# Transposes by DMA, smaller term buffers, deferred phi(q) and a fuller scheduler model in a two-layer attention kernel

## The chip, the cores and the metric

The kernel runs on one core of one Trainium2 chip. The metric is the device time of one execution in microseconds (us). All times are medians of several executions, with the lowest and highest in brackets where they matter.

The engines are named as in the profile: PE is TensorE (matmuls), PEld its weight loads, DVE is VectorE, ACT is ScalarE, POOL is GpSimd and SP the engine that issues DMAs here.

## The reference

Four blocks with residuals, A, B, A, B, on x of 2,048 rows by 512 columns in bf16:

```python
def _A_ref(x, wq, wk, wv, wo):        # 32 heads of 16, one shared key and value
    q = split_heads(x @ wq); k = x @ wk; v = x @ wv
    p = _softmax(q k^T * 16 ** -0.5)
    return merge_heads(p v) @ wo
def _B_ref(x, wqkv, wo):              # linear attention
    phi = lambda t: jnp.where(t > 0, t + 1, jnp.exp(t)) + 1e-6
    pq, pk = phi(q), phi(k)
    kv = einsum(pk, v); z = sum(pk)
    return merge_heads((pq kv) / (pq z + 1e-6)) @ wo
x = x + _A_ref(_layernorm(x), ...); x = x + _B_ref(_layernorm(x), ...)   # twice
```

(Notation shortened, meaning unchanged.) One A and the B after it are called a layer here. The softmax is nearly all of the work: 32 x 2,048 x 2,048 exponentials a layer, which the kernel cuts into 2,048 "positions" of 128 keys by 512 queries.

## The kernel before

The program orders its own instructions. Every operation is registered with an estimated duration, a priority, its buffers and the engines that may run it. A list scheduler plays the whole kernel through in a model at build time and writes down the order for each engine. The chip then follows that order, with semaphores.

The parts that matter (cuts marked by `# ...`):

```python
# the steady stage: two PSUM bank sets for ACT (banks 0-2 and 3-4), banks 5 and 6 for DVE,
# bank 7 for the accumulator; everything else ("misc") shares bank 6
def for_misc():
    # ...
    return (6, 5, 4, 3) if ctl.ramp else (6,)

# ACT: two or three positions by one exponential
oe = add(AC, tac(m * 512), lambda e: e.activation(PTA[...], bank(3 * s, m * 512), ACTF.Exp, scale=SCALE), ...)

# DVE: one position at a time out of PSUM (P1), then three shifted copies of four positions (xo);
# value matmuls with all four terms add up to the exponential
o = add(DV, tdv(512), lambda e: e.tensor_scalar(out=PTD[:, hp.idx, 0, i * 512:(i + 1) * 512], in0=bank(db), ...), name="P1")
dep = [add(DV, tdv(512 * m, 0.26), lambda e, r=r: e.tensor_scalar(out=PTD[:, hp.idx, r, 0:512 * m],
           in0=PTD[:, hp.idx, 0, 0:512 * m], scalar1=float(SHIFT[r]), ...), name="xo")]
# PTD: three buffers of 16 KB a partition, one for a group of four positions; free when all 16 matmuls are done

# layer norm, and the attention output likewise (otr, otc): transpose on PE, copy out of bank 6
o = add(PE, 0.22, tr, ..., acq=[hb], name="tr")                      # four 128x128 transposes
o2 = add((DV, AC), {...}, cp, uses=[hb], rel=[hb], name="xnT")       # copy to SBUF

# phi = max(t, 0) + min(exp t, 1): ACT, then DVE and POOL, then POOL adds
def phi(h, o, dst, keys, prio, tiled=False):
    o1 = add(AC, ..., ACTF.Exp, name="phe")
    o2 = add(DV, ..., op0=ALU.max, op1=ALU.add, name="phr")
    o3 = add(PO, PHM, ..., op0=ALU.min, op1=ALU.max, name="phm")
    add(PO, PHS, ..., op=ALU.add, name="phs")
```

The softmax here doesn't subtract the row's maximum and nothing guards it: scores larger than these inputs give would overflow.

## Time and profile before

1,659.47 us (1,656.86 to 1,660.10, three runs). From the timeline of ACT I cut the profiled execution (span 1,650.1 us) into five stages, at the first run of unbroken exponentials, at the end of the last exponential of each layer and at the first of the next.

| stage | us |
|---|---|
| start | 39.4 |
| plateau of layer one | 744.9 |
| change of layer | 54.3 |
| plateau of layer two | 760.2 |
| end | 51.3 |

In the lines of the groups view, the number after `x` is the count. After the first bar come the busy time of the group in us and the mean duration of one instruction in ns. After the second bar comes the idle time of the engine just before them, and what ended it. A line of the waits view reads: who waited, for whom, us in total, times, longest wait.

```profile
ACT PTA L845 <- PE ps_all L689: 62.7, 79, 10.5
DVE PTD L895 <- PE ps_all L689: 126.8, 222, 1.5
```

These are the two waits: ACT's exponential and DVE's conversion, each waiting for its score matmul.

### The profile page before, as it was taken

The numbers are of one execution on the slowest core, as the hardware profiler recorded it, in microseconds if no ns is written. First come the engines' busy times: TensorE is split into PE (matmuls) and PEld (weight loads), VectorE is DVE, ScalarE is ACT, GpSimd is POOL, SyncE is SP. The second block draws the span as 40 slices with busy tenths as digits, with TensorE's granted clock in tenths as the row PEclk, the third lists the DMA queues.
The fourth block names the chain that finished last, engine by engine and source line by source line (L and its number), as shares of the span: only waits on it lengthen the run. The fifth ranks groups of instructions, "written<-read, shape, count | busy, mean of one in ns | idle before, by whom it ended". The sixth has DMA issues, their size and how long they took to land.

```text
span 1650.1 us, 41487 instructions
## 1 busy us (share of the span) xinstructions
PE 1575.9 (96%) x18511; PEld 530.1 (32%) x18511; DVE 1434.9 (87%) x2536; ACT 1521.9 (92%) x1495; POOL 172.7 (10%) x222
## 2 busy tenths in 40 slices
PE   6999999999999899999799999999999998999998
PEld 4322223222333223333452232233223232333334
DVE  6999888899898889988689988888999988988976
ACT  6999999999999799999589999999999997999986
POOL 3000000100010101112210000001000102011131
PEclk9999999999999899999899999999999999999999
DMA  4000000000000000000000000000000000000001
GB/s 131 1 1 1 2 1 2 1 1 1 2 1 1 1 1 1 1 2 2 2 4 1 1 1 2 1 1 2 1 1 1 1 2 1 2 1 1 2 2 54
DMA packets 7779, 10.03 MB, mean 6 GB/s; under 512 B 1456, under 2 KB 7088, under 8 KB 7600
## 3 DMA queue, kind: packets, MB, share of 16 engines
q1 hardware_dynamic: 7600, 7.37, 1.4%
q8 instruction: 145, 2.38, 0.6%
q14 instruction: 34, 0.28, 0.1%
HBM read 5.28 MB, written 2.10 MB: 4 GB/s over the span
## 4 chain that ended last, share of the span: by engine, by line
PE 59%; ACT 20%; DVE 19%; issue 1%; DMA 0%; POOL 0%; SPq 0%
PE ps_all L689 23%; PE ps_all L726 23%; ACT PTA L845 19%; PE ps_all L460 10%; DVE PTD L895 7%; DVE PTD L912 6%; PE ps_all L747 2%; DVE Eo L738 1%; DVE e_buf L1022 1%; DVE stats L513 1%; PE ps_all L531 1%; DMA x_sb<-in_A_x_dram 0%; ACT e_buf L1021 0%; DVE v_tok L1042 0%; PE ps_all L997 0%
## 5 line engine op out<-in xcount | busy, mean ns | idle before, releaser
L845 ACT ACTIVATE PTA<-ps_all 128x1536 bf16<-128x1536 f32 (+1 forms) x1231 | 1422.9, 1276 | 66.9 <-PE ps_all L689 62.7
L895 DVE TENSOR_SCALAR PTD<-ps_all 128x512 uint16<-128x512 f32 x1005 | 680.6, 684 | 132.2 <-PE ps_all L689 126.8
L689 PE MATMUL ps_all<-QT,Kr 32*128 32x512 bf16 x4152 | 709.0, 384 | 22.4 <-ACT PTA L845 8.8
L726 PE MATMUL ps_all<-PTD,Vaug 128*32 128x512 bf16 x4020 | 584.6, 388 | 9.4 <-DVE Eo L738 7.2
L726 PE MATMUL ps_all<-PTA,Vaug 128*32 128x512 bf16 x3091 | 545.7, 388 | 0.7 <-ACT PTA L845 0.6
L912 DVE TENSOR_SCALAR PTD<-PTD 128x2048 uint16<-128x2048 uint16 x756 | 518.4, 704 | 4.7
L689 PEld LDWEIGHTS ps_all<-QT,Kr 32*128 32x128 bf16 x4152 | 176.5, 91 | 522.5 <-ACT PTA L845 214.0
L726 PEld LDWEIGHTS ps_all<-PTD,Vaug 128*32 128x32 bf16 x4020 | 143.5, 94 | 197.1 <-issue 127.5
L726 PEld LDWEIGHTS ps_all<-PTA,Vaug 128*32 128x32 bf16 x3091 | 132.0, 94 | 201.1 <-issue 169.7
L1024 POOL TENSOR_SCALAR e_buf<-e_buf 128x512 f32<-128x512 f32 x64 | 42.2, 660 | 597.6 <-ACT e_buf L1021 597.6
L521 POOL TENSOR_TENSOR rstd<-veps,mhalf 128x1 f32<-128x1 f32 x27 | 23.6, 873 | 743.9 <-DVE veps L519 733.9
L460 PE MATMUL ps_all<-wqkv_sb,xnT 128*32 128x512 bf16 x1024 | 85.1, 397 | 1.3 <-ACT xnT L537 0.8
L1022 DVE TENSOR_SCALAR e_buf<-ps_all 128x512 f32<-128x512 f32 x64 | 43.8, 684 | 21.9 <-ACT e_buf L1021 21.8
L1021 ACT ACTIVATE e_buf<-ps_all 128x512 f32<-128x512 f32 x64 | 39.9, 624 | 11.4 <-PE ps_all L460 8.7
L747 PE MATMUL ps_all<-identf,Eo 128*128 128x128 f32 x256 | 44.3, 298 | 5.6 <-DVE OT L1003 2.6
L460 PE MATMUL ps_all<-xnT,wq_sb 128*32 128x128 bf16 (+1 forms) x896 | 43.5, 303 | 5.2 <-issue 4.2
L513 DVE BATCH_NORM_STATS2 stats<-x_sb 128x6 f32<-128x512 bf16 x64 | 42.9, 679 | 4.5 <-DMA x_sb<-in_A_x_dram 2.9
L1027 POOL TENSOR_TENSOR pk_tok<-e_buf 128x512 bf16<-128x512 f32 x32 | 43.6, 1364 | 15.2 <-DVE e_buf L1022 15.0
L1027 POOL TENSOR_TENSOR pqT<-e_buf 128x512 bf16<-128x512 f32 x32 | 42.9, 1340 | 21.9 <-DVE e_buf L1022 21.2
L738 DVE COPY Eo<-ps_all 128x512 f32<-128x512 f32 x62 | 42.3, 682 | 2.8 <-PE ps_all L747 1.6
L460 PE MATMUL ps_all<-wo_sb,OT 128*32 128x512 bf16 x512 | 42.2, 382 | 1.7 <-issue 0.8
L460 PE MATMUL ps_all<-xnT,wqkv_sb 128*32 128x128 bf16 (+1 forms) x896 | 40.7, 292 | 0.6 <-DVE e_buf L1022 0.4
(83 smaller groups left out, 740.2 us busy)
## 6 DMA issues: line engine op xcount, KB each, us to landing
out_dram<-x_sb SPq DMA_DIRECT2D x16, 128.0 KB, 1.7
x_sb<-in_A_x_dram SPq DMA_DIRECT2D x3, 512.0 KB, 7.0
wqkv_sb<-in_B_wqkv_dram SPq DMA_DIRECT2D x1, 1536.0 KB, 11.9
x_sb<-in_A_x_dram SPq DMA_DIRECT2D x2, 256.0 KB, 3.3
wq_sb<-in_A_wq_dram SPq DMA_DIRECT2D x1, 512.0 KB, 5.1
wo_sb<-in_A_wo_dram SPq DMA_DIRECT2D x1, 512.0 KB, 8.6
wo_sb<-in_B_wo_dram SPq DMA_DIRECT2D x1, 512.0 KB, 11.4
wk_sb<-in_A_wk_dram SPq DMA_DIRECT2D x1, 16.0 KB, 2.6
```

The lines of the kernel that those rows point to most:

```text
L460: i = e.matmul(out[32 * c:32 * c + 32], lhsT=lhsT[:, 32 * c:32 * c + 32], rhs=rhs, start=start, stop=stop, skip_group_check=True)
L513: add(DV, tdv(512), lambda e: e.bn_stats(stats[:, t, 0:6], x_sb[:, t, :]), reads=[("x", t)], writes=[("st", t)], prio=prio, name="bn")
L689: x = e.matmul(bank(b0 + k), lhsT=Kr[r, m, kt * P:(kt + 1) * P], rhs=QT[r, self.units[u][0] % 2, gs, q0:q0 + n], start=True, stop=True)
L726: return e.matmul(ps[32 * c:32 * c + 32, 7 * 512:8 * 512], lhsT=Vaug[:, kt, r, :], rhs=src, start=opened[0], stop=opened[1], skip_group_ch ...
L738: return (e.copy if oe.eng == AC else e.tensor_copy)(Eo[:, he.idx, :], bank(7))
L747: i = e.transpose(bank(ht.idx, P, qs * P), Eo[:, he.idx, qs * P:(qs + 1) * P], identf[:])
L845: oe = add(AC, tac(m * 512), lambda e: e.activation(PTA[:, hp.idx, 0:m * 512], bank(3 * s, m * 512), ACTF.Exp, scale=SCALE), deps=[o] + pr ...
L895: o = add(DV, tdv(512), lambda e: e.tensor_scalar(out=PTD[:, hp.idx, 0, i * 512:(i + 1) * 512], in0=bank(db), scalar1=SCALE * LOG2E * 128. ...
L912: dep = [add(DV, tdv(512 * m, 0.26), lambda e, r=r: e.tensor_scalar(out=PTD[:, hp.idx, r, 0:512 * m], in0=PTD[:, hp.idx, 0, 0:512 * m], sc ...
L1022: o2 = add(DV, tdv(512), lambda e: e.tensor_scalar(out=e_buf[:, hr.idx, :], in0=bank(h.idx), scalar1=0.0, scalar2=1e-6, op0=ALU.max, op1=A ...
L1024: o3 = add(PO, PHM, lambda e: e.tensor_scalar(out=e_buf[:, he.idx, :], in0=e_buf[:, he.idx, :], scalar1=1.0, scalar2=0.0, op0=ALU.min, op1 ...
L1027: add(PO, PHS, lambda e: e.tensor_tensor(out=dst, in0=sh(e_buf[:, hr.idx, :]), in1=sh(e_buf[:, he.idx, :]), op=ALU.add), deps=[o2, o3], us ...
```

## The change

It has several parts. Transposes in the plateau leave PE and bank 6 and become DMAs from SBUF to SBUF. The shifted terms get 4 KB buffers of their own, given back term by term, and at most two groups of four positions are open at once (it was three). The two limits do not count the same thing: before, a group was open until all its 16 value matmuls were done; now it counts as open only until its first buffer is free, and its shifted terms may live on. The phi(q) blocks of query block 2 (`b` = 2, counted from 0) wait until the layer's exponentials are done. At the layer ends, phi is done in two DVE steps instead of the POOL chain, half the residuals are added by DVE instead of an identity matmul, and small steps may go to ACT. wq is loaded behind six x tiles. The scheduler's model learns that DVE's wide instructions and POOL exclude each other (`port`), and how long loads take. Some twenty priorities and limits get new values.

```diff
+NT0 = 2
+NPD = 12
+LX = 0.338
-MP, AP, MF, AF = 1, 2.0, 0.4, 2.0
+AP = 0.904
+MF = 0.758
+AF = 2.764
+PCONT = 0.992
... (more priorities)
+            if e == DV and o.port and self.tfree[PO] > self.now + 1e-9 or e == PO and self.dport > self.now + 1e-9:
+                continue
...
-    PTD = sb("PTD", [P, NPD, NTERM, 2048], U16)
+    PTD = sb("PTD", [P, NPD, 2048], U16)
...
+        late = not (ctl.ramp or ctl.tail or ctl.hot())
+        if late:
+            tdma(lambda e: [e.dma_start(xnT[:, ft, t * P:(t + 1) * P], xn_buf[:, hx.idx, ft * P:(ft + 1) * P], transpose=True) for ft in range(FT)], ...)
+            return
...
+        if not (ctl.tail or ctl.hot()):
+            tdma(lambda e: [e.dma_start(OT[...], Osb[:, hos.idx, k, :], transpose=True) for k in range(4)], ...)
...
-            if not self.ramp and sum(not o.done for o in self.p1s) < DMIN:
+            if not self.ramp and sum(not o.done for o in self.p1s) < DMIN and not (sc.tfree[AC] + LAT[AC] - now < LX and not all(banks.free[a] for a, w in SETS)):
...
-                if not p_ptd.free:
+                if not p_ptd.free or self.n0 >= NT0:
...
+        fast = (ctl.tail or ctl.hot()) and not slow      # phi: min and add on DVE, then max and add on DVE
...
+                    if b >= PQF:
+                        ctl.later.append((b, g))
...
+        own = t % 4 < YD                                 # residual by DVE, no identity matmul
```

The `LX` line keeps DVE's next score matmul back when ACT is about to run dry.

## The prediction

> **What bounds the kernel now.** The program's instruction order is fixed at build time by a list scheduler with a cost model; the chip only executes that order. Each attention layer has 2,048 units of 128 keys by 512 queries to exponentiate ("positions"), 4,096 in all, shared between ACT (true exponential, two or three positions per instruction) and DVE (a bit-pattern approximation: one conversion out of PSUM, then three shifted copies for four positions). I first read the busy shares and the 40 slices of the page.
>
> ```profile
> PE 1575.9 (96%) x18511; PEld 530.1 (32%) x18511; DVE 1434.9 (87%) x2536; ACT 1521.9 (92%) x1495; POOL 172.7 (10%) x222
> ...
> ACT  6999999999999799999589999999999997999986
> ...
> PEclk9999999999999899999899999999999999999999
> ```
>
> The reader is to see that no engine is plainly the bound: PE, ACT and DVE are all nearly full, in two long plateaus (one a layer) with ACT at 90% or more, and that there are five holes: the start, slice 14, the change of layer (slices 20 and 21), slice 34, the end. Then the groups of instructions, shapes kept apart, for the price of one position.
>
> ```profile
> L845 ACT ACTIVATE PTA<-ps_all 128x1536 bf16<-128x1536 f32 x630 | 933.5, 1482 | 57.6 <-PE ps_all L689 53.7
> L895 DVE TENSOR_SCALAR PTD<-ps_all 128x512 uint16<-128x512 f32 x1005 | 680.6, 684 | 132.2 <-PE ps_all L689 126.8
> L845 ACT ACTIVATE PTA<-ps_all 128x1024 bf16<-128x1024 f32 x600 | 636.7, 1061 | 9.3 <-PE ps_all L689 9.0
> L912 DVE TENSOR_SCALAR PTD<-PTD 128x2048 uint16<-128x2048 uint16 x753 | 517.8, 706 | 4.7
> ```
>
> ACT did 3,091 positions in 1,423 us of union time: 0.46 us each. DVE did 1,005 at 0.684 + 0.75 x 0.706 = 1.21 us. If DVE gets x us free it takes x/1.21 positions over, each worth 0.46 us of ACT; the time falls by x(0.46/1.67) = **0.275x**. A microsecond freed on ACT is worth 0.725. The same lines show that DVE idles 127 us for score matmuls and ACT 63 us: both wait for PE and for PSUM banks. In the steady stage one bank (6) serves every projection, transpose and normalization, and is also one of only two that feed DVE's conversions.
>
> Two of the holes I opened with the windows view (columns: window, length, busy PE, PEld, DVE, ACT, POOL with counts, granted clock).
>
> ```profile
> 560.00:565.00 5.00, 3.72 (x37) 0.98 (x40) 4.70 (x8) 5.00 (x6) 1.07 (x3) 1.00 0.01 3
> 565.00:570.00 5.00, 2.39 (x21) 0.68 (x13) 3.46 (x5) 0.66 (x2) 3.28 (x3) 0.52 0.00 0
> 570.00:575.00 5.00, 2.84 (x16) 1.56 (x16) 2.60 (x6) 0.00 (x0) 0.00 (x0) 0.50 0.00 0
> ...
> 1385.00:1390.00 5.00, 2.81 (x11) 1.22 (x11) 4.28 (x9) 0.74 (x2) 2.13 (x2) 0.78 0.00 0
> 1390.00:1395.00 5.00, 4.49 (x35) 1.51 (x36) 3.38 (x8) 1.45 (x1) 0.00 (x0) 0.54 0.00 0
> ```
>
> ACT is empty for some 10 us and the clock falls to half. The timeline says with what:
>
> ```profile
> 564.77 1.27 POOL L1027 TENSOR_TENSOR pqT<-e_buf 128x512 bf16<-128x512 f32 x1 [0.35 <-DVE e_buf L1022]
> ...
> 568.03 2.95 DVE L912 TENSOR_SCALAR PTD<-PTD 128x2048 uint16<-128x2048 uint16 x3
> ...
> 568.20 1.63 POOL L1027 TENSOR_TENSOR pqT<-e_buf 128x512 bf16<-128x512 f32 x1 [0.61 <-DVE e_buf L1022]
> ...
> 571.37 0.71 PEld L747 LDWEIGHTS ps_all<-identf,Eo 128*128 128x128 f32 x4 [2.86 <-DVE OT L1003]
> ...
> 577.38 1.45 ACT L845 ACTIVATE PTA<-ps_all 128x1536 bf16<-128x1536 f32 x1 [10.49 <-PE ps_all L689]
> ```
>
> The four phi(q) blocks of query block 2 hold bank 6 one after another, each until ACT and DVE have read it; behind them wait an output transpose, its DVE copy, and the transpose that frees the accumulator's evacuation buffer. Between 561 and 573 us no attention-times-value matmul runs at all.
>
> **What the Trainium skill says.** "SBUF — State Buffer", Who interferes with whom: DVE in a two-port mode (or with two SBUF inputs) and GpSimd exclude each other for a whole instruction. The trace agrees in kind: the 2,048-wide shift has a median of 0.684 and a maximum of 1.752 us, and three of them took 2.95 us beside POOL's addition. "TensorE: Matmul & The Clock Gate", Part 1: the clock is half when the array was idle for about a window of 3.4 us; the trace has 0.52 and 0.50 there. "VectorE: DVE Perf Modes", The three transpose paths: a full 128x128 bf16 transpose is 390 ns on TensorE and 1,309 ns by DMA. Here a TensorE transpose shows 219 ns; no transposing DMA is in this trace, so its cost is untested. "TensorEngine Tiling (Array Packing)", Key Properties: a change of tiling mode drains TensorE. The trace agrees: weight loads of a new form come after gaps of 0.23 or 0.42 us laid to "issue".
>
> **The change part by part.**
>
> (1) *DMA transposes.* 27 normalizations take the POOL power path, which marks the steady ones, and 29 output transposes were copied by DVE: up to 56, less the few in the last ten positions. Each loses four PE matmuls (0.40 us as a block, and about 0.2 us of tiling switch: 0.6) and a DVE copy of 0.418 us, and leaves bank 6 free for some 1.5 us. DVE: 54 x 0.418 = 22.6 us. PE: 54 x 0.6 = 32 us. SP gets 54 x 4 = 216 DMAs; it is idle in the plateaus, and even at the new model's 5.1 us for four it would be busy 275 of 1,500 us. Their latency lies on a chain (normalize, project, linear attention state) that has tens of us to spare until the layer's end, where TensorE is kept.
>
> (2) *phi(q) of block 2 put off.* Four blocks a layer leave the plateau: 8 x 0.624 = 5.0 us of ACT (worth 0.725: 3.6) and 8 x 0.684 = 5.5 us of DVE. They come back between the last exponential and the second half of the normalization tiles, where ACT is 31% and DVE 54% busy (790 to 810 us); 64 more matmuls are 3.5 us of PE a layer at full clock. Mostly hidden, I allow +1 us a layer.
>
> (3) *Holes 14 and 34.* ACT busy was 37.8 of 50 us (530 to 580) and 50.3 of 60 (1350 to 1410), against 96% elsewhere: 10.2 + 7.4 = 17.6 us. Parts 1 and 2 remove exactly the work that blocks bank 6 there. I take **15 us**.
>
> (4) *Port and load model, 4 KB term buffers.* The same 48 KB become 12 buffers of 4 KB that come free term by term. The DVE lane never shows a wait for a term buffer, only for PE, so I give this nothing by itself. Choosing non-port work while POOL runs saves at most 753 x (0.706 - 0.684) = 17 us of DVE; I take 10.
>
> (5) *Steady sums.* DVE freed: 22.6 + 5.5 + 10 = 38 us, x 0.275 = **10.5 us**; ACT **3.6 us**. PE's 32 us and the free bank shorten the waits: outside the holes ACT waits some 40 us for scores and DVE some 110; I take a third of each, 13 x 0.725 + 37 x 0.275 = **20 us**.
>
> (6) *Layer ends.* In the first, two late projection sets run after the last exponential (787 to 793 us) because bank 6 was crowded; with room they run before. POOL's 1.28 us addition leaves the chain (one 0.33 us estimated DVE step instead). Half the tiles drop the identity matmuls (0.21 us) for a DVE addition. I take 4 us a layer net of part 2: **8 us**. (7) *Start.* wq lands later, x earlier; odd tiles are scaled on POOL. First exponential now at 16.5 us, steady at 40: **2 us**.
>
> Sum: 15 + 10.5 + 3.6 + 20 + 8 + 2 = 59 us. 1659.5 - 59 = 1600.
>
> **Rivals.** *PE stays the wall.* PE is 98% busy in the plateaus, and each position moved to DVE costs it four value matmuls instead of one. Then parts 1 and 2 give only their PE time and the holes: 15 + about 15 + 8, near 1620. For it: the score loads wait for "issue" and switches. Against: ACT's waits for scores are under 5% of the plateau. *The DMA transpose becomes a new wait.* At several us, or with SP blocked in order behind a wait, normalized tiles arrive late, the backlog moves to the layer end, and up to 10 us come back in each: near 1630. Against: tens of us of slack. *The gain is larger.* The many three-digit priorities suggest a search; if ACT's remaining waits vanish (40 x 0.725 = 29 rather than 9) and DVE's too, 1565. *The model's better order collides elsewhere*: a new hole at another block boundary, -10 us of gain each.
>
> **Range and chances.** Holes and freed DVE and ACT time are counted (about 30 us); the waits, ends and start (30 us) are judged. So 1600, 8 in 10 between 1563 and 1630. Over 2% faster means under 1626: 0.87. Within 2%: 0.11. Slower: 0.02.
>
> **What would show it.** After: holes 14 and 34 gone and the clock at 1.00 there; DVE copies of xnT and OT down from 81 to about 27; conversions up from 1,005 to 1,070 or more; ACT's wait for scores well below 63 us; from the end of the last exponential of layer one (784.3 us) to the first of layer two (838.7 us) not longer than these 54 us. Wrong if conversions do not rise, if a wait for a transposing DMA appears on PE in the plateau, or if the layer ends grow by the phi(q) work.

## The result

1,572.46 us (1,565.83 to 1,577.25, four runs) against 1,658.16 us (four runs) of the kernel before. The ratio is 0.9489, with a 95% interval of 0.9441 to 0.9537. Ratios here are the mean time of one kernel's runs over that of the other's of the same rounds, so they are not quite the ratio of the medians.

The page of the changed kernel, the rows that answer to those of the prediction:

```profile
PE 1496.2 (96%) x18313; PEld 493.7 (32%) x18313; DVE 1433.3 (92%) x2556; ACT 1493.6 (95%) x1470; POOL 169.4 (11%) x229
...
ACT  6999999999999999999699999999999999999997
...
PEclk9999999999999999999999999999999999999999
```

The holes at slices 14 and 34 are gone, and besides the start and the end only one hole is left, the change of layer. The clock is full in all slices, but this is the fastest of the four executions: its mean clock was 1.000, that of the other three 0.989 to 0.993. PE and DVE are as full as before or fuller, and ACT too. The groups and waits of the changed kernel:

```profile
L903 ACT ACTIVATE PTA<-ps_all 128x1536 bf16<-128x1536 f32 x620 | 935.6, 1509 | 26.2 <-PE ps_all L746 23.8
L960 DVE TENSOR_SCALAR PTD<-ps_all 128x512 uint16<-128x512 f32 x1044 | 696.5, 685 | 64.9 <-PE ps_all L746 59.9
L1002 DVE TENSOR_SCALAR PTD<-PTD 128x2048 uint16<-128x2048 uint16 x783 | 525.1, 693 | 1.8
```

```profile
DVE PTD L960 <- PE ps_all L746: 59.9, 112, 1.4
ACT PTA L903 <- PE ps_all L746: 26.4, 45, 2.3
```

Both waits for scores have more than halved. DVE took 39 positions more (1,044 instead of 1,005). The new DMAs, from the page (line, count, median us from issue to landing):

```profile
OT<-Osb SPq DMA_TRANSPOSE x120, 2.4
xnT<-xn_buf SPq DMA_TRANSPOSE x120, 2.4
```

That is 60 blocks of four. The stages of the two profiled executions:

| stage | before | after | gain | predicted gain |
|---|---|---|---|---|
| start | 39.4 | 38.3 | 1.1 | 2 |
| two plateaus | 1,505.1 | 1,446.1 | 59.0 | 49 |
| change of layer and end | 105.6 | 79.7 | 25.9 | 8 |
| sum | 1,650.1 | 1,564.1 | 86.0 | 59 |

The prediction's sum came short by 27 us, and the larger part of that (18 us) is at the layer ends.

### The profile page after: what moved, and what is told of

Same layout as the page of the kernel before. It is cut to its first block, busy times and chain, and to the rows that moved or that the text cites. A ratio compares the mean times of both kernels' runs of the same rounds, so it can differ in the third digit from the quotient of the medians.

```text
span 1564.1 us, 41347 instructions
## 1 busy us (share of the span) xinstructions
PE 1496.2 (96%) x18313; PEld 493.7 (32%) x18313; DVE 1433.3 (92%) x2556; ACT 1493.6 (95%) x1470; POOL 169.4 (11%) x229
## 4 chain that ended last, share of the span: by engine, by line
PE 43%; ACT 43%; DVE 13%; issue 1%; DMA 0%; POOL 0%; SPq 0%
ACT PTA L903 41%; PE ps_all L746 16%; PE ps_all L783 16%; PE ps_all L495 9%; DVE PTD L960 5%; DVE PTD L1002 4%; PE ps_all L804 2%; DVE Eo L795 1%; ACT e_buf L1114 1%; DVE pqT L1244 1%; PE ps_all L586 0%; ACT e_buf L1242 0%; ACT e_buf L1243 0%; DVE x_sb L1259 0%; DVE x_sb L1106 0%
## 5 line engine op out<-in xcount | busy, mean ns | idle before, releaser
L903 ACT ACTIVATE PTA<-ps_all 128x1536 bf16<-128x1536 f32 (+1 forms) x1217 | 1401.8, 1303 | 29.3 <-PE ps_all L746 26.4
L960 DVE TENSOR_SCALAR PTD<-ps_all 128x512 uint16<-128x512 f32 x1044 | 696.5, 685 | 64.9 <-PE ps_all L746 59.9
L746 PE MATMUL ps_all<-QT,Kr 32*128 32x512 bf16 x4149 | 675.2, 383 | 25.1 <-ACT PTA L903 20.3
L1002 DVE TENSOR_SCALAR PTD<-PTD 128x2048 uint16<-128x2048 uint16 x783 | 525.1, 693 | 1.8
L783 PE MATMUL ps_all<-PTA,Vaug 128*32 128x512 bf16 x3052 | 522.0, 386 | 0.0
L746 PEld LDWEIGHTS ps_all<-QT,Kr 32*128 32x128 bf16 x4149 | 163.5, 91 | 514.9 <-ACT PTA L903 255.6
L783 PEld LDWEIGHTS ps_all<-PTD,Vaug 128*32 128x32 bf16 x4176 | 148.5, 94 | 191.9 <-issue 112.8
L783 PEld LDWEIGHTS ps_all<-PTA,Vaug 128*32 128x32 bf16 x3052 | 127.2, 94 | 203.2 <-issue 172.7
L563 POOL TENSOR_TENSOR rstd<-veps,mhalf 128x1 f32<-128x1 f32 x30 | 17.8, 594 | 848.5 <-DVE veps L561 848.5
L495 PE MATMUL ps_all<-wqkv_sb,xnT 128*32 128x512 bf16 x1024 | 73.9, 382 | 0.6 <-ACT xnT L592 0.5
L1121 DVE TENSOR_SCALAR e_buf<-ps_all 128x512 f32<-128x512 f32 x58 | 39.4, 683 | 3.5 <-ACT e_buf L1114 3.3
L495 PE MATMUL ps_all<-wo_sb,OT 128*32 128x512 bf16 x512 | 41.2, 382 | 0.1
```

The source lines that it names most:

```text
L495: i = e.matmul(out[32 * c:32 * c + 32], lhsT=lhsT[:, 32 * c:32 * c + 32], rhs=rhs, start=start, stop=stop, skip_group_check=True)
L746: x = e.matmul(bank(b0 + k), lhsT=Kr[r, m, kt * P:(kt + 1) * P], rhs=QT[r, self.units[u][0] % 2, gs, q0:q0 + n], start=True, stop=True)
L783: return e.matmul(ps[32 * c:32 * c + 32, 7 * 512:8 * 512], lhsT=Vaug[:, kt, r, :], rhs=src() if callable(src) else src, start=opened[0], s ...
L903: oe = add(AC, tac(m * 512), lambda e: e.activation(PTA[:, hp.idx, 0:m * 512], bank(SETS[s][0], m * 512), ACTF.Exp, scale=SCALE), deps=[o] ...
L1002: return e.tensor_scalar(out=PTD[:, ht.idx, 0:512 * m], in0=PTD[:, hp.idx, 0:512 * m], scalar1=float(SHIFT[r]), op0=ALU.add, **kw)
L1121: o2 = add(DV, tdv(512), lambda e: e.tensor_scalar(out=e_buf[:, hr.idx, :], in0=bank(h.idx), scalar1=0.0, scalar2=1e-6, op0=ALU.max, op1=A ...
```

## The experiments

Three theories were to be told apart. Theory A is the prediction's: the removed work and the freed bank are the gain, each by itself. Rival B says that the gain is the new order as a whole. Theory C, formed after the first four runs, says that removed work pays in the plateau only under an order that keeps ACT's scores in front.

"Plateaus" in the table is the end of the last exponential less the change of layer, less the same 39.4 us of start for all. It comes from the one profiled execution of each kernel, and these executions differ in their luck. The changed kernel's was 7 us faster than its median, u_phi_in_place's 11 and u_three_groups' 12 us faster, u_old_tail's 17 us slower. The granted clock was half for 45 us on end in the plateau of u_old_tail (350 to 395 us), so its plateau and its waits are too long here. So differences of some 10 us between the plateaus of single profiles prove nothing. "Waits" are for score matmuls.

| kernel | ratio to before | plateaus | change of layer | end | conversions | ACT waits | DVE waits |
|---|---|---|---|---|---|---|---|
| before | 1 | 1505.1 | 54.3 | 51.3 | 1005 | 62.7 | 126.8 |
| changed | 0.9489 | 1445.0 | 36.8 | 42.9 | 1044 | 26.4 | 59.9 |
| 1 f_dma_transposes | 0.9936 | 1504.5 | 48.8 | 46.4 | 1067 | 84.3 | 97.3 |
| 2 f_phi_later | 0.9960 | 1514.0 | 51.4 | 49.7 | 1004 | 70.9 | 133.7 |
| 3 u_pe_transposes | 0.9799 | 1491.2 | 39.6 | 47.6 | 991 | 46.8 | 116.4 |
| 4 c_pass (control) | 0.9597 | 1463.7 | 37.3 | 45.0 | 1034 | 38.0 | 75.7 |
| 5 u_old_prios | 0.9787 | 1490.1 | 36.4 | 44.6 | 1044 | 66.0 | 85.6 |
| 6 u_pe_old_prios | 0.9874 | 1513.7 | 36.6 | 44.5 | 999 | 70.2 | 126.8 |
| 7 u_three_groups | 0.9823 | 1476.3 | 55.8 | 42.3 | 1119 | 83.4 | 44.2 |
| 8 u_group_release | 0.9703 | 1479.6 | 40.0 | 49.6 | 1099 | 82.2 | 57.8 |
| 9 u_old_tail | 0.9593 | 1475.4 | 43.9 | 45.0 | 1035 | 48.4 | 89.2 |
| 10 u_phi_in_place | 0.9573 | 1457.6 | 34.3 | 40.6 | 1039 | 32.3 | 65.9 |
| 11 u_no_port_model | 0.9620 | 1468.0 | 38.9 | 44.3 | 1030 | 35.6 | 77.7 |
| 12 x_eo_dma | 0.9415 | 1431.3 | 35.3 | 44.9 | 1068 | 23.7 | 41.2 |

All twelve gave correct results. Numbers 1 to 4 were timed on one chip, the other batches on others, always beside the kernel before.

### 1. The DMA transposes alone (f_dma_transposes)

```diff
 # in the kernel before
+        if not (ctl.ramp or ctl.tail or ctl.pa + 10 >= len(ctl.pos)):
+            tdma(lambda e: [e.dma_start(xnT[...], xn_buf[...], transpose=True) for ft in range(FT)], ...); return
+        if not (ctl.tail or ctl.pa + 10 >= len(ctl.pos)):
+            tdma(lambda e: [e.dma_start(OT[...], Osb[...], transpose=True) for k in range(4)], ...)
```

> The kernel before with nothing but the steady transposes (xnT and OT) moved to DMA; old priorities, old group buffers, phi(q) in place. Theory A (removed work and a freed bank are the gain): about 35 of the 86 us, so 1623 us, ratio 0.979 to before; ACT's hole at slice 14 gone or under 4 us; conversions on DVE up from 1005 to 1060 or more. Rival B (the gain is the new order as a whole: priorities, mode batching, and no single removed work): at most 12 us, ratio 0.993 or more, and the hole stays.

Measured: 1,643.24 us, ratio 0.9936 (0.9897 to 0.9976). That is 0.6% instead of 2.1%, as rival B said. But the two things that theory A expected inside the run came true: 62 more positions on DVE (1,067), and the holes are gone. These are the stretches of holes 14 and 34 in this run (columns as in the prediction), where ACT was busy for 37.80 and 50.27 us before:

```profile
530.00:580.00 50.00, 49.37 (x485) 15.13 (x482) 43.96 (x76) 49.14 (x46) 8.58 (x8) 1.00 0.02 4
1350.00:1410.00 60.00, 57.85 (x552) 17.00 (x548) 59.41 (x102) 57.33 (x52) 1.88 (x2) 1.00 0.03 6
```

Four phi(q) blocks still run in the first of them (546 to 567 us). So under this order the DMA transposes alone were enough to close both holes. Yet ACT's waits for scores rose over the whole run from 62.7 to 84.3 us, and the plateaus were as long as before (1,504.5 against 1,505.1). New waits arose at other places, the longest at 1,012 us:

```profile
ACT PTA L854 <- PE ps_all L698: 84.3, 76, 6.6
```

```profile
1011.97 1.45 ACT L854 ACTIVATE PTA<-ps_all 128x1536 bf16<-128x1536 f32 x1 [6.59 <-PE ps_all L698]
```

This is what the prediction's last rival feared, a new hole at another place. What the run gained it gained at the layer ends: 54.3 + 51.3 became 48.8 + 46.4, 10.4 us. So taking this work off DVE, PE and bank 6 does not shorten the plateau by itself. This is the first result against theory A's exchange rate.

### 2. The deferral alone (f_phi_later)

```diff
 # in the kernel before
+                    if b >= 2:
+                        ctl.later.append((b, g))
```

> The kernel before with nothing but phi(q) of query block 2 put off to the layer's end. Theory A: the two holes (17 us of ACT) close and 5 us of ACT leave the plateau, the layer ends give some back: 15 us less, 1643 us, ratio 0.991. Rival B: within 5 us of before, ratio 0.997 to 1.003, a new hole somewhere else.

Measured: 1,647.85 us, ratio 0.9960 (0.9915 to 1.0005). The interval reaches 1, so no gain is shown. The hole is still there:

```profile
ACT PTA L849 <- PE ps_all L690: 70.9, 87, 10.2
```

The longest wait of ACT was 10.2 us, against 10.5 before. But the run does not test what it was built for. The four phi(q) blocks in front of the hole are still there, one to two us earlier than before:

```profile
563.82 1.27 POOL L1031 TENSOR_TENSOR pqT<-e_buf 128x512 bf16<-128x512 f32 x1 [0.35 <-DVE e_buf L1026]
...
566.57 1.63 POOL L1031 TENSOR_TENSOR pqT<-e_buf 128x512 bf16<-128x512 f32 x1 [0.38 <-DVE e_buf L1026]
```

They belong to query block 1, and neither this edit nor the change moves that block. Block 2's, which it does move, ran in the kernel before at 750 to 765 us, far from the hole, and in layer two nearly all at the end of the plateau or behind it (from 1,599 us). The prediction and I had taken the one block for the other. Whether block 1's phi(q) was needed for the hole in the old order was not tried. It is not enough to make one: number 1 and the changed kernel keep it in place (546 to 567 and 511 to 525 us) and have no hole there.

### 3. The changed kernel with its transposes back on PE (u_pe_transposes)

```diff
-        late = not (ctl.ramp or ctl.tail or ctl.hot())
+        late = False
-        if not (ctl.tail or ctl.hot()):
+        if False:
```

> The changed kernel with the transposes back on PE and their DVE copies back on bank 6. Theory A: 40 us slower than the changed kernel, about 1612 us, ratio 0.972 to before; conversions on DVE fall below 1010. Rival B: 15 us slower or less, 1587 us or less, ratio 0.957 or less.

Measured: 1,620.17 us, ratio 0.9799 (0.9766 to 0.9833). Against the changed kernel that is 0.9799/0.9489 = 1.033, some 50 us. Taken alone, the run is as theory A expected (40 us slower, conversions under 1,010; measured 991) and not as rival B did. But the same transposes that were worth 11 us in the kernel before are worth 50 here, or 33 against the control that follows. Neither theory predicts both.

### 4. A control (c_pass)

```diff
-SWITCH, PASS = 0.1, 0.217
+SWITCH, PASS = 0.1, 0.2175
```

> Control for the spread of schedules: the changed kernel with one constant of the scheduler's model moved by half a nanosecond (0.217 to 0.2175 us a pass), which changes no work but reshuffles the order. If the gain were luck of one order (the priorities look searched), this would lose much of it: 15 to 25 us slower than the changed kernel. If the work removed carries it, within 8 us of it, 1565 to 1580 us, ratio about 0.95.

Measured: 1,587.22 us, ratio 0.9597 (0.9567 to 0.9627), so 1.1% slower than the changed kernel for a change of half a nanosecond in the model. No operation was added or taken away, only the order differs (and with it the share of DVE, 1,034 conversions instead of 1,044). The loss is 15 us by the medians and 18 by the ratios, beyond the 8 us that the expectation allowed for removed work alone. So some 15 to 18 us of the 86 are the luck, or the fitting, of one order. Undoing a part costs about that much whatever the part is, and **a loss of up to about 1.1% against the changed kernel proves nothing about the part undone.** This is one control, not a distribution. Three later edits, numbers 9 to 11, landed near it too (0.9573 to 0.9620).

### 5 and 6. The order, and the fourth corner (u_old_prios, u_pe_old_prios)

```diff
 # changed kernel, all its work kept
-AP = 0.904
-MF = 0.758
-AF = 2.764
-PCONT = 0.992
-PX = 2.241
-EVP = 1.348
-LX = 0.338
+AP = 2.0
+MF = 0.4
+AF = 2.0
+PCONT = 1.5
+PX = 3.0
+EVP = 2.1
+LX = -9.0        # no guard for ACT's scores
... (PQP, PB, PY, PKV, PTR, PZ and LEAD2 likewise; number 6 has number 3's edit as well)
```

> The changed kernel with the scheduler's old priorities, old limits for changing PE's tiling mode and no guard for ACT's scores; all work as in the changed kernel (DMA transposes, put-off phi(q), small buffers, short layer end). Theory C (removed work pays only under an order that keeps ACT's scores in front): 35 to 50 us slower than the changed kernel, near 1615, ACT's waits for scores up from 26 us to 60 or more while DVE's conversions stay above 1040. Theory A (removed work pays by itself): not worse than the control's 15 us, so under 1590.

> Fourth corner of transposes x order: transposes on PE and old priorities, everything else as in the changed kernel (put-off phi(q), small buffers, port model, short layer end). Known corners: DMA and new order 1572, PE and new order 1620, DMA and old order 1618. Theory C (the two need each other): the missing corner is only slightly slower than those two, 1625 to 1640. Additive theory (each worth 46 to 48 us alone): 1660 or more, no faster than the kernel before.

Measured: 1,618.25 us, ratio 0.9787 (0.9755 to 0.9819), and 1,633.47 us, ratio 0.9874 (0.9847 to 0.9901). The waits view of u_old_prios:

```profile
ACT PTA L903 <- PE ps_all L746: 66.0, 83, 3.1
```

It has exactly as many conversions as the changed kernel (1,044), yet ACT's waits are back at 66 us. The four corners, with everything else as in the changed kernel:

| | old order | new order |
|---|---|---|
| transposes on PE | 0.9874, plateaus 1513.7 | 0.9799, plateaus 1491.2 |
| transposes by DMA | 0.9787, plateaus 1490.1 | 0.9489, plateaus 1445.0 |

Starting from the corner of PE and old order, the new order alone gives 0.8%, the DMAs alone 0.9%, both together 3.9%. In the plateaus that is 22, 24 and 69 us. The surplus over the sum is 2.2% of the time, as theory C says, and the fourth corner is not at the 1,660 us that the additive theory expected.

A large reservation belongs here. The new values look fitted to the changed kernel with its DMAs, and the other three corners are not fitted. With the control (0.9597, plateaus 1463.7) in place of the changed kernel the surplus is 1.1%, no more than the control itself lost, and in the plateaus it is gone: 22 and 24 us singly, 50 together. So three things have to be kept apart. That the DMAs and the new order each count is shown: without either, the kernel is 3% slower, 2% more than the control explains. That each counts for less without the other (0.8 and 0.9%) is measured. That they need each other, and are not only fitted to each other, is not shown: for that the constants would have to be fitted to the kernel with its transposes on PE as well. Which of the 14 constants carries it was not tried on the chip either.

### 7 and 8. How many groups DVE may open (u_three_groups, u_group_release)

```diff
 # u_three_groups
-NT0 = 2
+NT0 = 3
 # u_group_release: the same, and a term's buffer is given back only when all four terms are done
-                            sc.at(o_.vis, lambda: p_ptd.give(src.idx, None))
+                            done(o_, src)      # collects; gives all four back at the end
```

> The changed kernel with its fine buffers but three open groups allowed on DVE, as before the change, instead of two. With groupwise release and three groups the kernel took 1604, with 1099 conversions and 82 us of ACT waits. If the third group alone does that (DVE sends single-position score matmuls ahead of ACT's): 1598 or more, conversions over 1090, ACT waits over 60 us. If it was the groupwise release: within 15 us of the changed kernel, under 1588.

> The changed kernel with term buffers of the same size given back only when a whole group of four terms is done, three groups at most, as before. My prediction gave the finer buffers nothing: within the control's 15 us, under 1590. If they matter, DVE conversions change by more than 30 and the time rises by 20 us or more, over 1592.

Measured: 1,627.15 us, ratio 0.9823 (0.9779 to 0.9867), and 1,604.46 us, ratio 0.9703 (0.9674 to 0.9733). One constant costs 3.5% against the changed kernel. Because of the new way of counting open groups, number 7 is looser than the kernel before ever was; number 8, which lost 2.3%, is the old rule. The groups and the wait in u_three_groups:

```profile
L960 DVE TENSOR_SCALAR PTD<-ps_all 128x512 uint16<-128x512 f32 x1119 | 743.0, 682 | 48.2 <-PE ps_all L746 44.2
...
ACT PTA L903 <- PE ps_all L746: 83.4, 82, 5.2
```

DVE did 75 positions more than in the changed kernel and ACT's waits tripled. A position on DVE needs four value matmuls instead of one (4,476 against 4,176 in the changed kernel), and a score pass of its own. So the likely reading is that a DVE that is allowed more takes PE from ACT; the count alone does not decide it, for number 12 did 1,068 conversions with ACT waits of 23.7 us. Groupwise release throttled DVE again (1,099) and lost less. The small buffers were thus not the cause of a gain by themselves: with three groups, fine release (and a looser limit) was worse than groupwise release. Two groups with groupwise release were not tried.

The rest of the loss is at the change of layer, 55.8 us, and its chain shows a thing that I had named as a rival (start us, length us, what):

```profile
777.09 1.23 SPq L579
...
778.36 2.00 SPq L579
...
780.41 3.69 DMA xnT<-xn_buf
...
784.23 1.93 PE ps_all L495 x32
```

Here a normalization came too early for the switch back to PE, and its transposing DMA lay on the chain of the layer end for 7.1 us (777.0 to 784.1). In the changed kernel itself no such line appears: its waits name a DMA only for x at the start.

### 9. The old layer end (u_old_tail)

```diff
-        fast = (ctl.tail or ctl.hot()) and not slow
+        fast = False
-YD = 2
+YD = 0
-                    zo[g] = add((AC, DV), ...)
+                    zo[g] = add(DV, ...)
```

> The changed kernel with the old work at the layer ends: phi always through POOL, all residuals by identity matmuls on PE, zb on DVE alone. The layer change took 54.3 us before and 36.8 after, the end 51.3 and 43.0. If the shorter chain of work is the cause: both come back by half or more, layer change 45 us or more, and 12 to 20 us slower in all (1585 to 1592). If it is the freed bank that lets late projections run before the end: layer change stays under 41 us and the time within the control's 15 us.

Measured: 1,588.89 us (1,583.14 to 1,605.73), ratio 0.9593 (0.9557 to 0.9629), which the control alone explains. But the stage itself can be read: the change of layer took 43.9 us instead of 36.8. Its chain ran over POOL:

```profile
779.13 1.05 issue
780.18 1.32 POOL pqT L1125
781.50 0.59 POOL e_buf L1123
782.09 0.07 issue
782.16 0.74 POOL pqT L1125
```

In the changed kernel the same place is two DVE instructions:

```profile
761.52 0.61 ACT e_buf L1114
...
762.15 0.96 DVE e_buf L1116
763.11 0.60 DVE pk_tok L1118
```

So of the 25.9 us gained at the layer ends, the shorter chain accounts for 7.1 at the change of layer and 2.1 at the end, by this one profile. The stage ran there at a mean clock of 0.96, against 1.00 in the changed kernel, so a part of the 7.1 can be the clock. The first test of my expectation (45 us or more) was missed by one us, the second (under 41) by three, and the rest of the 25.9 stays partly open. The DMA transposes alone gave 10.4 us there in the kernel before, the deferral 4.5 us. These do not add up cleanly: the fourth corner has a change of layer of 36.6 us with its transposes on PE.

What that corner does show is that the whole of its gain over the kernel before is at the layer ends. It has 17.7 and 6.8 us less there, and plateaus no shorter (1,513.7). So the gain at the layer ends needs neither the DMAs nor the new order.

### 10 and 11. Two parts that cannot be seen (u_phi_in_place, u_no_port_model)

```diff
 # u_phi_in_place
-PQF = 2
+PQF = 4
 # u_no_port_model
-            if e == DV and o.port and self.tfree[PO] > self.now + 1e-9 or e == PO and self.dport > self.now + 1e-9:
+            if False:
```

> The changed kernel with all phi(q) blocks computed where they become ready. Theory A gives them 5 us of ACT and a part of the holes: 8 to 12 us slower than the changed kernel, 1582. The rival that the holes come from bank 6 and POOL, which the DMA transposes already relieve: 0 to 5 us beyond what the control lost, so within 1572 to 1590, and no ACT wait above 3 us.

> The changed kernel ordered by a scheduler that does not know that DVE's two-port instructions and POOL exclude each other; the chip still does. If the port model is worth what I predicted (10 us of DVE, 3 us of time): within the control's 15 us, under 1590. If the collisions derail the order as in the old holes: over 1595, mean of the 2,048-wide shifts back above 700 ns and ACT waits of 5 us or more.

Measured: ratios 0.9573 (0.9534 to 0.9613) and 0.9620 (0.9593 to 0.9647). Against the changed kernel that is 0.9% and 1.4%, beside the control's 1.1%. Neither part is shown to be worth anything. Number 10 fits both of its expectations (1,584.18 us). Number 11 (1,590.14 us) lies between its two. The deferral even lengthens the two layer ends by some 5 us in the profiles (36.8 + 42.9 against 34.3 + 40.6).

Without the port model the wide shift took 706 ns again instead of 693, so the model does keep DVE and POOL apart. 783 x 13 ns is 10 us of DVE, as predicted, but the end of the program does not show it.

### 12. One more transpose moved (x_eo_dma)

If PE's time and bank 6 are worth time under the new order, the remaining transposes of the plateau should go too. They turn the accumulator around, 256 fp32 matmuls in 64 blocks. 62 of the blocks were moved.

```diff
-    Eo = sb("Eo", [P, 2, 512], FP32)
+    Eo = sb("Eo", [P, NEB, 512], BF16)
+    Et = sb("Et", [P, NET, 4, P], BF16)
...
+            if late:
+                o = tdma(lambda e: [e.dma_start(Et[:, ht.idx, qs, :], Eo[:, he.idx, qs * P:(qs + 1) * P], transpose=True) for qs in range(4)], ...)
 # and seven constants (LX, HOLD, MF, AF, EVX, HOT, three buffers for Eo) refitted
```

> A version meant to beat both: the changed kernel, with the last transposes of the plateau moved too. The accumulator is copied out as bf16 instead of fp32 and transposed by DMA (on PE in bf16 near a layer's end), so 64 blocks of four fp32 transposes on PE (0.59 us each, 38 us in all) and 64 holdings of bank 6 go; seven constants of the scheduler are fitted to that work. Theory C (with ACT's scores in front, PE time and bank 6 are worth time): 10 to 25 us faster than the changed kernel, 1547 to 1562, ratio 0.935 to 0.944 to before; ACT's waits for scores stay near 26 us, conversions rise above 1055. Rival (PE is no longer what limits the plateau, or the accumulator's longer way through DMA stalls the value matmuls): within 6 us of the changed kernel or slower, over 1566. Outputs still within tolerance; if not, the bf16 accumulator copy is too coarse.

Measured: 1,556.18 us (1,552.58 to 1,558.48, six runs), ratio 0.9415 (0.9390 to 0.9441), correct.

```profile
ACT PTA L917 <- PE ps_all L751: 23.7, 39, 2.6
DVE PTD L974 <- PE ps_all L751: 41.2, 85, 1.4
```

It is the fastest of all: 0.9415/0.9489 = 0.992 of the changed kernel, by two comparisons with the kernel before whose intervals just touch. The two were not timed in the same rounds. DVE's waits fell by another 19 us, its conversions rose to 1,068, ACT's waits did not rise, and the plateaus are 14 us shorter. Because the constants were refitted with the new work, the run does not separate the two.

## Why the prediction was right, and where its working was wrong

The time lay within the range (1,563 to 1,630) and the direction was as given. Step by step:

- **What bounds the kernel** held. All three engines are nearly full, and what costs time are ACT's and DVE's waits for PE. The changed kernel removed 36 of ACT's 63 us and 67 of DVE's 127 us.
- **Holes 14 and 34** (15 us) are gone and the clock is 1.00 there, as predicted, but half of the reason was wrong. The four phi(q) blocks in front of hole 14 are of query block 1, not 2, and the change does not defer them. Of the two parts that were to close the holes, the DMA transposes did it alone (number 1, ACT busy 49.14 of 50 us), and the deferral could not. Part 2 was over-counted too: in layer two block 2's phi(q) had hardly been in the plateau at all.
- **The exchange rate 0.275x** is the step that failed for the removed work by itself. It takes for granted that ACT, with less to do, is fed in time. Number 1 moved 62 positions and took 30 us of work from ACT (busy 1,521.9 to 1,492.0), and the plateaus did not shorten, because ACT waited longer. Number 7 moved 75 more than the changed kernel and lost 3.5%. In mechanism my first rival, "PE stays the wall", was closer there, though its time (near 1,620) was further off.
- **The conversions** rose by 39, and 1,070 or more were expected. That figure does not follow from the working. With the 75 us that it frees on DVE and the 17 us on ACT outside the holes, its own balance moves (75 - 17) / 1.67 = 35 positions. Only the 75 us divided by 1.21 (62 positions) come near it, as if ACT gained no time at all. So the 39 agree with the rate.
- **A third of each wait** (20 us) was too careful: more than half of both went. It took both the order and the freed PE; without the one or the other ACT waited for 66.0 or 46.8 us.
- **Nothing for the small buffers**, because no wait for a buffer was seen, missed that the same lines change the limit of open groups. The old rule (number 8) costs 32 us in the changed kernel, about half of it beyond the control. It was in the diff and not in my working.
- **The port model**: 10 us of DVE predicted, 10 us measured, with no effect on the end that the control does not explain.
- **Layer ends** (8 us) were mis-sized by a factor of three: 25.9 us. Of it, at most 9 us are traced to the shorter phi, residual and zb steps. 24.5 us are there without the DMAs and the new order (number 6). What makes up the rest is not settled.
- **The DMA as a new wait** did not come true in the changed kernel, but it did in number 7, for 7.1 us on the chain.
- **DVE copies of xnT and OT** fell from 81 to 21 (27 predicted), since 60 blocks moved instead of 54.

The prediction was thus right in time partly by luck, by errors that cancel: work taken away was credited at a rate that it does not earn by itself, and the order, the limit of open groups and the layer ends were credited too little or not at all.

## What to carry to other kernels

Where three engines are full, price a piece of work by what it takes from the engine that the others wait for, not by the rate of the engine that gets free. A helper that is let do more can slow the whole, as number 7 did, when its work costs the shared engine more. Before crediting one part of a change to a scheduled program, run a control that changes only the order, since here half a nanosecond in the model was worth 1.1%. Try pairs: work taken off PE and a new order were worth under 1% each and 3.9% together. But fit the order for every corner before you call the surplus real: against the control it is 2.8%. And check in the trace that an edit moved the work that you meant, since number 2 moved another block.

## What the Trainium skill lacked or had wrong

- "VectorE: DVE Perf Modes", The three transpose paths: it gives 390 ns for a 128x128 bf16 transpose on TensorE, where the trace has 219 ns for one matmul and 0.40 us for a block of four. For DMA it gives one figure, 1,309 ns. Here, SBUF to SBUF, a transposing DMA of a normalized tile held the issuing queue for 1,233 ns (median; 1,094 to 2,207) and landed 2.4 us after issue (median), so four took 4.9 us to issue. The page does not part the two, and the scheduling needs both.
- "DMA: Bandwidth & Descriptors", DMA Transpose (X-bar): no number of packets. 240 transposes brought the packets of the hardware queue from 7,600 to 46,000, which is 160 each, and the queue's share of the DMA engines from 1.4% to 4.0%. No wait of a compute engine in the plateau of the changed kernel names one of them.
- "SBUF — State Buffer", Who interferes with whom: its rule agrees in kind, but it has no measure of how little it can matter. The wide shift's mean was 706 ns before, 706 without the port model and 693 with it, and the time did not show it beyond the control.
- "TensorE: Matmul & The Clock Gate", Part 1: its table gives half the clock after an idle window of about 3.4 us. The traces differ, and the prediction's reading of the hole with it. In the kernel before, the clock fell at 565.2 us, though PE was busy for 2.1 of the 3.4 us before that and its longest gap was 0.8 us. In u_old_tail it stayed at 0.50 from 350 to 395 us, with PE shown as busy all the time (ends of matmuls are modelled). Part 1 speaks of drops from short idle gaps for another kernel, but does not say how much idle time it takes.
